# Gated linear attention into a three-way maxout FFN: weights by the fp32 queue in order of use with casts on three engines, the state update as its own stage, and a ring of one-bank PSUM slots

## The chip, the cores and the metric

The kernel runs on one core of one Trainium2 chip. Times are device microseconds of one execution. A run's time is 1.7 to 1.9 us longer than the span of its profile, which counts from the first to the last instruction. Executions of one kernel mostly agree within 1%. Engines are named as the profile names them: PE is TensorE's matrix multiplication (PEld its weight loads), DVE the vector engine, ACT the scalar engine, POOL the GpSimd engine, SP the engine that issues most transfers.

## The reference

```python
batch, n_heads, seq, head_dim = (4, 8, 768, 48)       # q, k, v, alpha
n_tokens, d_model, d_ff = (3072, 384, 768)            # w1, w2, w3, w_out

def _attn_ref(q, k, v, alpha):
    state = np.zeros((B, H, D, D)); y = np.zeros_like(q)
    for t in range(S):
        state = alpha[:, :, t, :, None] * state + np.einsum('bhd,bhe->bhde', k[:, :, t], v[:, :, t])
        y[:, :, t] = np.einsum('bhd,bhde->bhe', q[:, :, t], state)
    return y

def _moe_ref(x, w1, w2, w3, w_out):                   # x: y as tokens x 384
    h = np.maximum(np.maximum(x @ w1, x @ w2), x @ w3)
    return h @ w_out
```

Everything is given and returned in fp32; the kernel multiplies in fp16.

## The kernel before

Work is cut into 12 **units** of two batches by 128 tokens (all 8 heads): two pairs of batches by six blocks of time, the pairs in turn, so the state that a unit leaves is needed two units later. Each unit passes four steps, and I use these names throughout:

- **A**: logarithm of alpha (ACT), sums over time by matmul (`lps`), exponentials (ACT), and k, q, v scaled (POOL, DVE).
- **B**: k and q transposed on TensorE (`tps`) and copied by DVE (`qkT`), the score products k·q (`aps`), masked by DVE (`lat`), the outputs (`yps`), and their transposition (`xtp`).
- **C**: the new state (`sps`), multiplied by a product of gates (`gm`) into `st`. Before the change this is inside B.
- **FFN**: 54 matmuls of 256 columns (`gps`), two casts by ACT and two maxima by DVE for each third (`h`, `hT`), then 12 matmuls of 384 columns (`ops`).

PSUM is the memory that this kernel's matmuls write their results to; a slot is a piece of it that tiles of one tag take in turn. The kernel divides PSUM into four one-bank slots for `gps` (tag "g"), two for `xtp`, `yps`, `sps`, `ops` (tag "s"), and two more banks as ONE slot (tag "w") that `lps`, `tps` and `aps` share.

```python
    def load_weights():                       # POOL's queue; the transfer converts fp32 to fp16
        for jg in range(NJ // 2):
            for g, w in enumerate((moe_w1, moe_w2, moe_w3)):
                cs = slice(jg * 2 * P, (jg + 1) * 2 * P)
                nc.gpsimd.dma_start(
                    wcat[:, :, g, cs], w.rearrange("(f p) j -> p f j", p=P)[:, :, cs])
        nc.gpsimd.dma_start(wo16, moe_w_out.rearrange("(j p) m -> p j m", p=P))
# ... (stage_a cut)
    def stage_b(s):
        tps = ps.tile([P, 2 * NP, P], FP16, name="tps", tag="w", bufs=1)
        for i in range(2 * NP):
            nc.tensor.transpose(tps[:, i, :], qkf[:, i, :], ident)
        nc.vector.tensor_copy(out=qkT.rearrange("p i a t -> p (i a) t"), in_=tps)
        # ...
            for i in range(2):                # gate products
                nc.vector.scalar_tensor_tensor(
                    out=gm[:, :, i], in0=gate_of[s][:, :, 1], scalar=half_c[i],
                    in1=gate_of[s + B // U][:, :, 0], op0=AOP.mult, op1=AOP.mult)
        for u in range(U):                    # two batches
            aps = ps.tile([P, 2, HP, P], FP32, name="aps", tag="w", bufs=1)
            for p in range(HP):               # four pairs of heads
                for i in range(2):            # rows 0 to 47, rows 64 to 111
                    rows = slice(64 * i, 64 * i + D)
                    nc.tensor.matmul(aps[:, i, p, :], qkT[rows, 1, u * HP + p, :],
                                     qkT[rows, 0, u * HP + p, :], start=True, stop=True)
            # ... mask, yps, xb, xtp, and the state (sps, st)
# ...
    stage_a(0)
    load(1)
    load_weights()
    load(2)
    stage_a(1)
    stage_a(2)
    stage_b(0)
    for s in range(NS):
        if s + 3 < NS:
            load(s + 3)
            stage_a(s + 3)
        if s + 1 < NS:
            stage_b(s + 1)
        ffn(s)
```

The order in which an engine meets its instructions is set when the program is built, from this source and from which slots are free; it can differ from the source's order, and "program order" below means that built order. I read the traces as each engine taking its instructions in order; unit 0's transposes, below, are an example.

Of the kernel before, what the change touches and what calls it, by code (L numbers as in the profile page):

```python
# [12 lines left out]
AOP = mybir.AluOpType  # L13
# [10 lines left out]
def kernel(  # L24
# [43 lines left out]
    raw = ctx.enter_context(tc.tile_pool(name="raw", bufs=3))  # L68
# [12 lines left out]
    def load(s):  # L81
        cb, b0 = where(s)
        for n in ("a", "q", "k", "v"):
            t = raw.tile([P, NH, D], FP32, name=f"r{n}", tag=f"r{n}")
            nc.sync.dma_start(  # L85
                t, ins[n][cb * P:(cb + 1) * P, b0:b0 + U].rearrange("s b h d -> s (b h) d"))
            raws[s, n] = t
# [8 lines left out]
    half_c = (c32[:, 4:5], c32[:, 5:6])  # L96
# [5 lines left out]
    for i in range(NQ):  # L102
        nc.vector.memset(las[i], 0.0)
        nc.gpsimd.memset(qks[i], 0.0)
    sts = [[cpool.tile([P, HP, 2 * D], FP16, name=f"st{b}_{i}") for i in range(2)]
           for b in range(B)]

    wcat = cpool.tile([P, NF, 3, DF], FP16, name="wcat")
    wo16 = cpool.tile([P, NJ, DM], FP16, name="wo16")

    def load_weights():
        for jg in range(NJ // 2):
            for g, w in enumerate((moe_w1, moe_w2, moe_w3)):
                cs = slice(jg * 2 * P, (jg + 1) * 2 * P)
                nc.gpsimd.dma_start(
                    wcat[:, :, g, cs], w.rearrange("(f p) j -> p f j", p=P)[:, :, cs])
        nc.gpsimd.dma_start(wo16, moe_w_out.rearrange("(j p) m -> p j m", p=P))
# [3 lines left out]
    def stage_a(s):  # L121

        la, qk = las[s % NQ], qks[s % NQ]
        nc.scalar.activation(  # L124
            out=la.rearrange("p a b c -> p (a b) c")[:, :, :D], in_=raws.pop((s, "a")),
            func=AFT.Ln)
        lps = ps.tile([P, 2, 512], FP32, name="lps", tag="w", bufs=1)
        laf = la.rearrange("p a b c -> p (a b) c")
        for i in range(2):
            nc.tensor.matmul(lps[:, i, :H * D], tri, laf[:, i * H:(i + 1) * H, :D],  # L130
                             start=True, stop=True)
        for p in range(NP):
            nc.tensor.matmul(lps[:, 0, H * D + 2 * p:H * D + 2 * p + 2],  # L133
                             la[:, p].rearrange("p a b -> p (a b)"), w2,
                             start=True, stop=True)
        ac = work.tile([P, 2, H, D], FP32, name="ac", tag="ac")
        ic = work.tile([P, 2, H, D], FP32, name="ic", tag="ic")
        ge = work.tile([P, NP, 2], FP32, name="ge", tag="ge", bufs=6)
        lv = lps[:, :, :H * D].rearrange("p i (h d) -> p i h d", d=D)
        nc.scalar.activation(out=ac, in_=lv, func=AFT.Exp, bias=at_c, scale=1.0)  # L140
        nc.scalar.activation(out=ic, in_=lv, func=AFT.Exp, bias=nat_c, scale=-1.0)  # L141
        nc.scalar.activation(  # L142
            out=ge, in_=lps[:, 0, H * D:H * D + 2 * NP].rearrange("p (a b) -> p a b", b=2),
            func=AFT.Exp)
        gate_of[s] = ge
        qv, kv = (qk[:, i].rearrange("p a b c -> p (a b) c")[:, :, :D] for i in range(2))
        nc.vector.tensor_mul(qv, raws.pop((s, "q")), ac.rearrange("p i h d -> p (i h) d"))  # L147
        nc.gpsimd.tensor_mul(kv, raws.pop((s, "k")), ic.rearrange("p i h d -> p (i h) d"))  # L148
        vt = work.tile([P, NH, D], FP16, name="vt", tag="vt", bufs=4)
        nc.gpsimd.tensor_scalar_mul(vt, raws.pop((s, "v")), vs_c)  # L150
        qk_of[s], v_of[s] = qk, vt

    def stage_b(s):

        cb, b0 = where(s)
        qk, vt = qk_of.pop(s), v_of.pop(s)
        qkf = qk.rearrange("p i a b c -> p (i a) (b c)")
        tps = ps.tile([P, 2 * NP, P], FP16, name="tps", tag="w", bufs=1)
        for i in range(2 * NP):
            nc.tensor.transpose(tps[:, i, :], qkf[:, i, :], ident)  # L160
        qkT = work.tile([P, 2, NP, P], FP16, name="qkT", tag="qkT")
        nc.vector.tensor_copy(out=qkT.rearrange("p i a t -> p (i a) t"), in_=tps)  # L162
        xT = work.tile([P, NF, U, P], FP16, name="xT", tag="xT")
        xtp = ps.tile([P, U, NF, P], FP16, name="xtp", tag="s", bufs=2)
        gm = None
        if cb + 1 < NCB:
            gm = work.tile([P, NP, 2], FP32, name="gm", tag="gm")
            for i in range(2):
                nc.vector.scalar_tensor_tensor(  # L169
                    out=gm[:, :, i], in0=gate_of[s][:, :, 1], scalar=half_c[i],  # L170
                    in1=gate_of[s + B // U][:, :, 0], op0=AOP.mult, op1=AOP.mult)
        for u in range(U):
            b = b0 + u
            st, stn = sts[b][cb % 2], sts[b][(cb + 1) % 2]
            aps = ps.tile([P, 2, HP, P], FP32, name="aps", tag="w", bufs=1)
            for p in range(HP):
                for i in range(2):
                    rows = slice(64 * i, 64 * i + D)
                    nc.tensor.matmul(aps[:, i, p, :], qkT[rows, 1, u * HP + p, :],  # L179
                                     qkT[rows, 0, u * HP + p, :], start=True, stop=True)  # L180
            la_ = work.tile([P, 2, HP, P], FP16, name="lat", tag="lat")
            nc.vector.tensor_mul(  # L182
                la_.rearrange("p i a t -> p (i a) t"), aps.rearrange("p i a t -> p (i a) t"),
                mask.unsqueeze(1).broadcast_to([P, H, P]))
            yps = ps.tile([P, HP, 2, D], FP32, name="yps", tag="s", bufs=2)
            for p in range(HP):
                if cb > 0:
                    nc.tensor.matmul(yps[:, p], qkT[:, 0, u * HP + p, :], st[:, p, :],  # L188
                                     start=True, stop=False)
# [8 lines left out]
            if cb + 1 < NCB:  # L198
                sps = ps.tile([P, HP, 2, D], FP32, name="sps", tag="s", bufs=2)
                if cb > 0:  # L200
                    nc.tensor.matmul(sps.rearrange("p a b d -> p (a b d)"), ident,
                                     st.rearrange("p a b -> p (a b)"),
                                     start=True, stop=False)
                for p in range(HP):
                    nc.tensor.matmul(  # L205
                        sps[:, p], qkf[:, NP + u * HP + p, :],
                        vt[:, u * H + 2 * p:u * H + 2 * p + 2, :],
                        start=(cb == 0), stop=(cb == 0 or p == HP - 1))
                nc.vector.tensor_mul(
                    stn.rearrange("p a (b d) -> p a b d", d=D), sps,  # L210
                    gm[:, u * HP:(u + 1) * HP, :].unsqueeze(3).broadcast_to([P, HP, 2, D]))
        nc.scalar.copy(out=xT.rearrange("p f u t -> p u f t"), in_=xtp)
        xT_of[s] = xT

# [33 lines left out]
    stage_a(0)  # L248
    load(1)
    load_weights()  # L250
    load(2)
    stage_a(1)
    stage_a(2)
    stage_b(0)
    for s in range(NS):
        if s + 3 < NS:
            load(s + 3)
            stage_a(s + 3)
        if s + 1 < NS:
            stage_b(s + 1)  # L260
        ffn(s)
# [30 lines left out]
```

## Time and profile before

| | before |
|---|---|
| median of its runs (three, when the prediction was made) | 212.29 us (210.94 to 212.34) |
| span of the profile | 209.7 us |
| first FFN product starts | 47.6 us |
| end of FFN(0), FFN(4), FFN(11) | 61.5, 118.3, 206.0 us |
| one full iteration (mean of four, 105.5 to 161.8 us) | 14.08 us |

From the page of before, the busy shares, the overview (40 slices of 5.24 us; a digit is the busy share in tenths, PEclk the granted clock of TensorE in tenths) and the chain of waits:

```profile
PE 154.2 (74%) x1736; PEld 117.1 (56%) x1736; DVE 120.9 (58%) x164; ACT 104.1 (50%) x181; POOL 63.2 (30%) x42
...
PE   0110002469997989987699877899988999999992
...
PEclk9999999999999999999999999999999999999998
DMA  7999999999109959889179689500200102020012
...
SPq L85 8%; PE ops L241 7%; DMA ra<-in_alpha_dram 7%; DVE gm L169 4%; ACT xb L195 4%; ACT ac L140 3%; PE tps L160 3%; PE xtp L197 3%; DVE hT L237 3%; DVE qkT L162 3%; PE aps L179 3%; DVE lat L182 2%; PE yps L191 2%; PE yps L188 2%; PE sps L205 1%
```

TensorE does almost nothing for seven slices (37 us) while the transfer engines are full; two slices later it is 60 to over 90% busy. The order of time of TensorE at the end of that stretch (start, time, engine, line, operation, tile, count, and in brackets the idle time before and who ended it):

```profile
33.34 0.80 PE L130 MATMUL lps<-la_82,c_68 128*128 128x384 f16 x2 [18.26 <-ACT la_82 L124]
...
36.18 1.87 PE L160 MATMUL tps<-c_68,qk_84 128*128 128x128 f16 x16 [1.85 <-ACT ge L142]
...
47.62 0.37 PE L226 MATMUL gps_403<-xT,wcat 128*128 128x256 f16 x1 [0.65 <-ACT xT L212]
```

TensorE waits 18 us for the sums of unit 2, whose alpha lands at 32.4 us; unit 0's transposes, whose data are long there, stand behind them in the queue. The stretches of four later iterations (length, then busy time and number of instructions of PE, PEld, DVE, ACT and POOL, granted clock, share of the transfer engines, GB/s):

```profile
105.50:118.30 12.80, 12.03 (x141) 9.06 (x139) 8.21 (x11) 6.88 (x13) 3.60 (x2) 1.00 0.89 186
118.30:134.40 16.10, 13.23 (x161) 10.12 (x160) 11.54 (x17) 10.81 (x19) 4.37 (x3) 1.00 0.87 173
134.40:146.80 12.40, 11.98 (x140) 9.04 (x138) 7.86 (x11) 6.18 (x11) 3.63 (x2) 1.00 0.09 33
146.80:161.80 15.00, 13.21 (x163) 10.20 (x161) 12.13 (x16) 9.69 (x18) 2.80 (x2) 1.00 0.08 28
```

TensorE is busy 50.45 of these 56.3 us, so an iteration holds 12.6 us of it and 1.5 us of waits.

### The profile page before, as it was taken

To read this page: it belongs to the slowest core of one execution; us is meant where nothing else is said; L and a number is where in the kernel's file an instruction comes from. 1 tells how busy PE (TensorE), PEld (TensorE's weight loads), DVE (VectorE), ACT (ScalarE), POOL (GpSimd) and SP (SyncE) were. 2 spreads that over 40 slices of the span, in tenths; PEclk is the share of its full clock that TensorE was granted. 3 is DMA by queue.
4 is the path that set the end of the run, shared out by engine and by line. 5 is a ranking of instruction groups with operands and counts; after the bars stand their busy time and mean duration, and the time that the engine had idled before them with its cause. 6 is when DMAs were issued, how large, how long until landed. Compare 5 with 4: busy or idle time off the path is not lost.

```text
span 209.7 us, 4208 instructions
## 1 busy us (share of the span) xinstructions
PE 154.2 (74%) x1736; PEld 117.1 (56%) x1736; DVE 120.9 (58%) x164; ACT 104.1 (50%) x181; POOL 63.2 (30%) x42
## 2 busy tenths in 40 slices
PE   0110002469997989987699877899988999999992
PEld 0110002347676767675487665676766777767680
DVE  3101002755939888479857398475798865548250
ACT  2422004073567574684656556645748454644651
POOL 8997313607403434052330430704303000000000
PEclk9999999999999999999999999999999999999998
DMA  7999999999109959889179689500200102020012
GB/s 140 218 189 219 178 201 230 218 220 204 31 27 237 222 122 224 155 200 223 31 179 193 139 179 231 124 16 3 78 0 23 55 3 75 5 75 3 27 48 75
DMA packets 107219, 26.32 MB, mean 126 GB/s; under 512 B 99776, under 2 KB 107200, under 8 KB 107200
## 3 DMA queue, kind: packets, MB, share of 16 engines
q1 hardware_dynamic: 102528, 23.60, 56.9%
q0 software_dynamic: 4384, 2.36, 8.0%
q8 instruction: 13, 0.21, 0.4%
q10 hardware_dynamic: 288, 0.10, 0.3%
q14 instruction: 6, 0.05, 0.1%
HBM read 23.69 MB, written 4.72 MB: 136 GB/s over the span
## 4 chain that ended last, share of the span: by engine, by line
PE 45%; DVE 18%; ACT 15%; SPq 8%; DMA 7%; issue 5%; ACTq 0%; DVEq 0%
SPq L85 8%; PE ops L241 7%; DMA ra<-in_alpha_dram 7%; DVE gm L169 4%; ACT xb L195 4%; ACT ac L140 3%; PE tps L160 3%; PE xtp L197 3%; DVE hT L237 3%; DVE qkT L162 3%; PE aps L179 3%; DVE lat L182 2%; PE yps L191 2%; PE yps L188 2%; PE sps L205 1%
## 5 line engine op out<-in xcount | busy, mean ns | idle before, releaser
L226 PEld LDWEIGHTS <-wcat 128*128 128x128 f16 x648 | 60.1, 99 | 7.6
L150 POOL TENSOR_SCALAR vt<-rv,c_69 128x768 f16<-128x768 f32 x12 | 26.5, 2205 | 43.7 <-DMA rv<-in_v_dram 21.2
L182 DVE TENSOR_TENSOR lat<-aps,c_68 128x1024 f16<-128x1024 f32 x24 | 29.2, 1219 | 5.7 <-PE aps L179 5.7
L241 PE MATMUL ops<-wo_105,hT 128*128 128x384 f16 x144 | 26.7, 326 | 4.5 <-DVE hT L237 1.7
L241 PEld LDWEIGHTS <-hT 128*128 128x128 f16 x144 | 13.4, 98 | 14.7 <-DVE hT L237 4.7
L130 PEld LDWEIGHTS <-c_68 128*128 128x128 f16 x24 | 2.2, 100 | 32.4 <-issue 27.4
L244 ACT COPY ob<-ops 128x384 f32<-128x384 f32 x24 | 11.1, 480 | 17.9 <-PE ops L241 17.8
L162 DVE COPY qkT<-tps 128x2048 f16<-128x2048 f16 x12 | 14.6, 1220 | 8.6 <-PE tps L160 8.6
L195 ACT ACTIVATE xb<-yps,c_69 128x384 f16<-128x384 f32 x24 | 14.0, 582 | 10.9 <-PE yps L191 10.7
L169 DVE SCALAR_TENSOR_TENSOR gm<-ge,c_69 128x8 f32<-128x8 f32 x20 | 16.5, 862 | 1.3 <-ACT ge L142 1.1
L130 PE MATMUL lps<-la_82,c_68 128*128 128x384 f16 x6 | 1.8, 385 | 18.3 <-ACT la_82 L124 18.3
L147 DVE TENSOR_TENSOR qk_86<-rq,ac 128x768 f16<-128x768 f32 x3 | 2.9, 958 | 20.7 <-ACT ac L140 20.7
L140 ACT ACTIVATE ac<-lps,c_69 128x768 f32<-128x768 f32 x12 | 10.9, 905 | 7.1 <-PE lps L133 7.1
L179 PE MATMUL aps<-qkT 48*128 48x128 f16 x192 | 10.0, 226 | 6.0 <-DVE qkT L162 5.9
L191 PE MATMUL yps<-vt,lat 128*128 128x48 f16 x192 | 11.6, 187 | 1.6 <-DVE lat L182 1.5
L148 POOL TENSOR_TENSOR qk_87<-rk,ic 128x768 f16<-128x768 f32 x3 | 5.4, 1810 | 24.1 <-ACT ic L141 14.3
L197 PE MATMUL xtp<-c_68,xb 128*128 128x128 f16 x72 | 8.5, 229 | 5.0 <-ACT xb L195 3.3
L191 PEld LDWEIGHTS <-lat 128*128 128x128 f16 x192 | 9.6, 98 | 4.1 <-DVE lat L182 3.0
L179 PEld LDWEIGHTS <-qkT 48*128 48x128 f16 x192 | 5.6, 97 | 9.7 <-DVE qkT L162 9.0
L141 ACT ACTIVATE ic<-lps,c_69 128x768 f32<-128x768 f32 x12 | 10.8, 904 | 0.0
L124 ACT ACTIVATE la_82<-ra 128x768 f16<-128x768 f32 x3 | 2.6, 850 | 15.6 <-DMA ra<-in_alpha_dram 15.6
L197 PEld LDWEIGHTS <-xb 128*128 128x128 f16 x72 | 4.2, 100 | 10.7 <-ACT xb L195 10.5
(331 smaller groups left out, 333.0 us busy)
## 6 DMA issues: line engine op xcount, KB each, us to landing
ra<-in_alpha_dram SPq DMA_DIRECT2D x12, 384.0 KB, 5.7
rq<-in_q_dram SPq DMA_DIRECT2D x12, 384.0 KB, 5.7
rk<-in_k_dram SPq DMA_DIRECT2D x12, 384.0 KB, 5.7
rv<-in_v_dram SPq DMA_DIRECT2D x12, 384.0 KB, 5.8
out_dram<-ob SPq DMA_DIRECT2D x24, 192.0 KB, 1.9
wcat<-in_moe_w_dram POOLq DMA_DIRECT2D x9, 192.0 KB, 6.1
wo_105<-in_moe_w_out_dram POOLq DMA_DIRECT2D x1, 576.0 KB, 11.5
c_68<-c ACTq DMA_DIRECT2D x1, 96.5 KB, 2.7
```

The lines of the kernel that those rows point to most:

```text
L85: nc.sync.dma_start(t, ins[n][cb * P:(cb + 1) * P, b0:b0 + U].rearrange("s b h d -> s (b h) d"))
L140: nc.scalar.activation(out=ac, in_=lv, func=AFT.Exp, bias=at_c, scale=1.0)
L150: nc.gpsimd.tensor_scalar_mul(vt, raws.pop((s, "v")), vs_c)
L162: nc.vector.tensor_copy(out=qkT.rearrange("p i a t -> p (i a) t"), in_=tps)
L169: nc.vector.scalar_tensor_tensor(out=gm[:, :, i], in0=gate_of[s][:, :, 1], scalar=half_c[i], in1=gate_of[s + B // U][:, :, 0], op0=AOP.mul ...
L179: nc.tensor.matmul(aps[:, i, p, :], qkT[rows, 1, u * HP + p, :], qkT[rows, 0, u * HP + p, :], start=True, stop=True)
L182: nc.vector.tensor_mul(la_.rearrange("p i a t -> p (i a) t"), aps.rearrange("p i a t -> p (i a) t"), mask.unsqueeze(1).broadcast_to([P, H, ...
L191: nc.tensor.matmul(yps[:, p, i, :], la_[:, i, p, :], vt[:, u * H + 2 * p + i, :], start=(cb == 0), stop=(cb == 0 or i == 1))
L195: nc.scalar.mul(xb, yps.rearrange("p a b d -> p (a b d)"), ys_c)
L197: nc.tensor.transpose(xtp[:, u, f, :], xb[:, f * P:(f + 1) * P], ident)
L226: nc.tensor.matmul(gps[:, j, :], wcat[:, f, g, jj * P:(jj + 1) * P], xT[:, f].rearrange("p u t -> p (u t)"), start=(f == 0), stop=(f == NF ...
L241: nc.tensor.matmul(ops, hT[:, jj, u * P:(u + 1) * P], wo16[:, jj, :], start=(jj == 0), stop=(jj == NJ - 1))
```

## The change

Its intent: (1) stage B(0) and FFN(0) no longer stand behind three stages A and all loads; weights come in fp32 by the same queue as the inputs, cut in the order in which FFN(0) uses them, and ACT, DVE and POOL share the casts; (2) the state update is a stage C of its own, and its gate products go from DVE to POOL; (3) the two-bank slot becomes a ring of two one-bank slots, so that TensorE can fill one while DVE empties the other.

```diff
@@ weights
-                nc.gpsimd.dma_start(
-                    wcat[:, :, g, cs], w.rearrange("(f p) j -> p f j", p=P)[:, :, cs])
-        nc.gpsimd.dma_start(wo16, moe_w_out.rearrange("(j p) m -> p j m", p=P))
+                t = cpool.tile([P, NF, 2 * P], FP32, name=f"ws{jg}_{g}")
+                nc.sync.dma_start(t, w.rearrange("(f p) j -> p f j", p=P)[:, :, cs])
+                wstage.append((g, wcat[:, :, g, cs], t))
+        # ... w_out in three parts likewise; g = 0, 1, 2 is cast by ACT, DVE, POOL
@@ stage_a: one-bank sums per batch instead of one two-bank tile
-        lps = ps.tile([P, 2, 512], FP32, name="lps", tag="w", bufs=1)
+        for u in range(U):
+            lps = ps.tile([P, 512], FP32, name="lps", tag="w", bufs=2)
+            # ... sums, exponentials, and k, q scaled, per batch
@@ stage_b
-        tps = ps.tile([P, 2 * NP, P], FP16, name="tps", tag="w", bufs=1)
+        for u in range(U):
+            tps = ps.tile([P, 2, HP, P], FP16, name="tps", tag="w", bufs=2)
+            # ... eight transposes, one copy
-            aps = ps.tile([P, 2, HP, P], FP32, name="aps", tag="w", bufs=1)
+            aps = [ps.tile([P, HP, P], FP32, name=f"aps{i}", tag="w", bufs=2)
+                   for i in range(2)]
             for p in range(HP):
                 for i in range(2):
                     rows = slice(64 * i, 64 * i + D)
-                    nc.tensor.matmul(aps[:, i, p, :], qkT[rows, 1, u * HP + p, :], ...
+                    nc.tensor.matmul(aps[i][:, p, :], qkT[rows, u, 1, p, :], ...
+            for i in range(2):                    # two half masks instead of one
+                nc.vector.tensor_mul(la_[:, i], aps[i], mask...)
@@ stage_c, new: the state update, out of stage_b
+        gt = work.tile([P, NP], FP32, name="gt", tag="gt")
+        nc.gpsimd.tensor_mul(gt, gate_of[s][:, :, 1], gate_of[s + B // U][:, :, 0])
+        gm = work.tile([P, NP, 2], FP32, name="gm", tag="gm")
+        nc.gpsimd.tensor_mul(gm, gt..., half_c...)
+        # ... sps and st as before
@@ order
-    stage_a(0)
     load(1)
     load_weights()
     load(2)
+    load(3)
+    stage_a(0)
+    stage_b(0)
     stage_a(1)
-    stage_a(2)
-    stage_b(0)
+    cast_weights()
     for s in range(NS):
-        if s + 3 < NS:
-            load(s + 3)
-            stage_a(s + 3)
+        if s + 4 < NS:
+            load(s + 4)
         if s + 1 < NS:
             stage_b(s + 1)
+        if s + 2 < NS:
+            stage_a(s + 2)
+        stage_c(s)
         ffn(s)
```

(Also: k is loaded ahead of q, four input buffers instead of three, only the padding is cleared.)

## The prediction

> **What bounds the kernel now.** The 40-slice overview shows two regimes. Until about 47 us TensorE is mostly idle: the stretch table gives it 2.0 of the first 18 us, 0.7 of the next 16. Later it is the limit: 13.6 of 14 us at 160 to 174. The chain of waits explains the start: SyncE's issue of loads (8%), then 14.3 us for the third unit's alpha, until 32.45. The program queues stage A of units 0, 1 and 2 on TensorE ahead of the first stage B, so the first transposes, whose data were there by 13 us, run at 34.5 to 38, and the first FFN matmul at 47.6. An iteration with stage A takes 13.5 to 15 us, the last ones 11.7 to 12. In the order of time at 134.3 to 147.2 I count 12.2 us of real TensorE work in a full iteration, so 1.5 to 2 us are waits.
>
> **What changes.**
> 1. Start. Only unit 0's load precedes stage B(0); then unit 1; then weights. Before, units 0, 1 and all weights had landed by about 31 us, and the same bytes are read now, so I keep 32 us for the last weight. The Trainium skill ("DMA: Bandwidth & Descriptors", Issuing engines are not separate DMA queues) says all queues share the same 16 engines; the trace agrees: DMA share 0.9 or more in this time. The gain is not bandwidth but what TensorE does meanwhile: A(0), B(0), A(1), B(1), FFN(0)'s first products; FFN(1) stands ahead of unit 2.
> 2. Twelve casts of 128x768. The like-sized ACT logarithm takes 0.85 us, POOL's scaling 2.2: 4 us each on ACT, DVE, 6 to 9 on POOL, inside the load time, off the chain.
> 3. DVE loses the gate products (1.85 us a unit, 16.5 in all), which stand before the transposes' copy on the chain. POOL gets two small ones.
> 4. PSUM ring: two one-bank slots instead of one of two banks; copy and masks halved (1.22 us becomes 2 x 0.65), so TensorE fills one while DVE empties the other. State products leave the ring between the two heads' outputs.
> 5. ACT gets three more instructions per unit, some 0.5 us.
>
> TensorE's work is unchanged (3,474 rows in both orders).
>
> **Sum.** At 32 us FFN(0)'s first products are done. Left: one output product 2.1, 11 FFN at 8.05, ten B at 2.8, ten A at 0.55, ten C at 0.66: 131 us. Waits: 0.75 us x 11 = 8 (0.55 of each before the last output products: unchanged); 2 us of slow clock (early transposes take 117 ns, later 66); 7 us in units 2 to 4, whose stage B has no FFN matmuls between its steps; 3.7 after the last matmul. Span 184; the time runs 1 to 2.6 above: **185 us, range 177 to 193**. Faster by over 2%: 0.96; within: 0.03; slower: 0.01.
>
> **Right if:** first FFN matmul before 25 us, FFN(1)'s before 35; full iterations of 12.6 to 13.4 us; TensorE's busy share above 82%; last weight landed at 29 to 36 us; no gate products on DVE.
>
> **Wrong if:** weights land after 36 us; in-order casts hold up stage B; loads of units 2 to 5, now behind 4.7 MB of weights, starve TensorE at 40 to 60 us; POOL's casts slow down beside DVE's; or halved steps add more fixed cost than overlap, leaving iterations at 14 us (then about 194).

## The result, and the profile after

| | before | predicted | after |
|---|---|---|---|
| median | 212.31 us (4 runs) | 185 (177 to 193) | 197.27 us (196.82 to 197.89, 4 runs) |
| span of the profile | 209.7 | 184 | 195.0 |
| first FFN product | 47.6 | under 25 | 23.3 us |
| FFN(0)'s 54 products done | 59.1 | 32 | 35.4 us |
| end of FFN(4) | 118.3 | 95.6 (the same terms) | 101.9 us |
| full iteration | 14.08 | 12.8 | 13.86 us (five, from FFN(4) to FFN(9)) |
| last weight landed | 30.5 | 32 | 31.9 us |

The ratio to before is 0.930, 95% interval 0.924 to 0.936. Ratios here are the mean time of one kernel's fast runs over the mean of the other's fast runs of the same rounds, so they are not quite the ratios of the medians that I quote.

The change is faster by 7%, but 12 us slower than I said. FFN(4) ends 16.4 us earlier than before, FFN(11) 14.3 us: all of the gain is made at the start, and later iterations cost nearly what they did. The lines of the page that answer to those of before:

```profile
PE 167.9 (86%) x1736; PEld 122.5 (63%) x1736; DVE 116.8 (60%) x200; ACT 110.7 (57%) x221; POOL 61.2 (31%) x64
...
PE   0295886958869979999989999999989999999992
...
PEclk9999999996999988999999999999999999999999
DMA  7999999999996059379699909819720020020102
...
PE ops L267 7%; DVE hT L263 5%; PE tps L179 5%; ACT ic L157 4%; DMA rq<-in_q_dram 3%; SPq L85 3%; DMA ra<-in_alpha_dram 2%; ACT xb L208 2%; POOL vt L167 2%; POOL qk_86 L163 2%; ACT ac L158 2%; PE yps L204 2%; POOL gt L221 1%; DVE qkT L182 1%; PE xtp L210 1%
```

The first line is the surprise. TensorE runs the same 1,736 matmuls, and is busy 13.7 us longer. The gate products of DVE (4% of the old chain) are gone from it; the POOL that took them is in it.

The order of time of TensorE at the start, in after:

```profile
23.32 0.82 PE L252 MATMUL gps_437<-xT,wcat 128*128 128x256 f16 x3
...
32.55 0.83 PE L252 MATMUL gps_491<-xT,wcat 128*128 128x256 f16 x6 [0.75 <-ACT wcat L131]
33.94 0.83 PE L252 MATMUL gps_498<-xT,wcat 128*128 128x256 f16 x6 [0.55 <-DVE wcat L133]
...
44.43 3.72 PE L267 MATMUL ops<-wo_97,hT 128*128 128x384 f16 x12 [2.59 <-DVE st_1_89 L237]
```

FFN(0) starts when predicted, but waits for casts (2.0 us in all, with one at 28.8 and one at 30.2 us), although the weight behind the line at 32.55 had landed at 26.4 us: ACT made its cast at 31.66, in program order behind its own casts of FFN(0)'s products. FFN(0)'s last part, `ops`, comes 9 us after its products: it needs an output slot, and both are held by state products that wait for a gate of unit 2. Its 12 matmuls then take 3.7 us instead of 2.1.

The stretches of five full iterations in after:

```profile
101.90:115.80 13.90, 13.39 (x151) 9.71 (x149) 9.61 (x16) 8.71 (x19) 4.91 (x5) 1.00 0.75 156
115.80:129.40 13.60, 13.42 (x152) 9.75 (x150) 9.23 (x16) 9.77 (x20) 4.90 (x5) 1.00 0.68 146
129.40:144.30 14.90, 13.65 (x157) 10.11 (x155) 9.37 (x16) 8.74 (x19) 7.03 (x6) 1.00 0.68 135
144.30:157.60 13.30, 13.11 (x147) 9.46 (x145) 9.22 (x16) 8.33 (x18) 2.72 (x4) 1.00 0.08 31
157.60:171.20 13.60, 13.41 (x152) 9.75 (x150) 9.22 (x16) 8.28 (x18) 2.72 (x4) 1.00 0.08 30
```

Waits have nearly gone, as intended, but TensorE is now busy 13.4 us in each. To see with what, I added up every matmul's time from its start to the next one's start, less the gap after its recorded end (that gap is the wait). Per full iteration, in us; the last column is an experiment below:

| | predicted | before | after | all scores together |
|---|---|---|---|---|
| FFN products and outputs | 8.05 | 8.50 | 8.69 | 8.57 |
| B | 2.8 | 2.83 | 3.51 | 3.02 |
| of B, the scores `aps` | | 0.66 | 1.31 | 0.66 |
| A | 0.55 | 0.56 | 0.54 | 0.53 |
| C | 0.66 | 0.75 | 0.66 | 0.66 |
| waits | 0.75 | 1.46 | 0.46 | 1.10 |
| sum | 12.81 | 14.10 | 13.86 | 13.88 |

The scores take double the time with the same 16 matmuls. In before they come as two groups of eight, in after as four groups of four. A group of eight in before, then groups of four in after:

```profile
107.72 0.40 PE L179 MATMUL aps<-qkT 48*128 48x128 f16 x8
108.05 0.22 PE L188 MATMUL yps<-st_0_100,qkT 128*128 128x96 f16 x1
```

```profile
117.08 0.39 PE L193 MATMUL aps_1788<-qkT 48*128 48x128 f16 x4
117.40 0.22 PE L201 MATMUL yps<-st_1_93,qkT 128*128 128x96 f16 x1
...
117.88 0.40 PE L193 MATMUL aps_1789<-qkT 48*128 48x128 f16 x4
118.21 0.61 PE L252 MATMUL gps_1906<-xT,wcat 128*128 128x256 f16 x4
```

From the start of each group to the next matmul 0.32 to 0.33 us pass. A group of eight takes as long (108.05 less 107.72, and again in the first experiment). Each matmul uses 48 of the 128 rows, one half of the array; with both halves in one tile they run side by side, and with a one-bank tile for each half, in a ring of two slots, program order parts the halves. The Trainium skill ("TensorEngine Tiling (Array Packing)", Key Properties) says that tiles work independently and can multiply in parallel, and that "Changing tiling mode (not just tile) drains the TensorE". The traces agree as far as they go: in the group of eight two matmuls start 3 or 4 ns apart and the next two some 55 ns later, in the group of four each starts some 55 ns after the one before; in both, 0.15 us pass from the last start to the next product. That this last part is the draining, no run shows. Twice as many groups, twice the time.

So my **first theory** was: the time missing in full iterations is TensorE's, made by the parted scores (0.65 us an iteration, 6.5 us over ten), and the time missing at the start comes from the output slots held by C(0). The **rival**: TensorE's time is not what sets an iteration; waits would take the place of whatever it saved.

### The profile page after: what moved, and what is told of

Same layout as the page of the kernel before. It is cut to its first block, busy times and chain, and to the rows that moved or that the text cites. A ratio compares the mean times of both kernels' runs of the same rounds, so it can differ in the third digit from the quotient of the medians.

```text
span 195.0 us, 4340 instructions
## 1 busy us (share of the span) xinstructions
PE 167.9 (86%) x1736; PEld 122.5 (63%) x1736; DVE 116.8 (60%) x200; ACT 110.7 (57%) x221; POOL 61.2 (31%) x64
## 3 DMA queue, kind: packets, MB, share of 16 engines
q1 hardware_dynamic: 106944, 28.32, 67.5%
## 4 chain that ended last, share of the span: by engine, by line
PE 41%; DVE 16%; ACT 13%; issue 9%; POOL 9%; DMA 5%; SPq 4%; POOLq 0%; DVEq 0%; ACTq 0%
PE ops L267 7%; DVE hT L263 5%; PE tps L179 5%; ACT ic L157 4%; DMA rq<-in_q_dram 3%; SPq L85 3%; DMA ra<-in_alpha_dram 2%; ACT xb L208 2%; POOL vt L167 2%; POOL qk_86 L163 2%; ACT ac L158 2%; PE yps L204 2%; POOL gt L221 1%; DVE qkT L182 1%; PE xtp L210 1%
## 5 line engine op out<-in xcount | busy, mean ns | idle before, releaser
L267 PE MATMUL ops<-wo_97,hT 128*128 128x384 f16 x144 | 29.2, 342 | 6.1 <-DVE hT L263 2.9
L267 PEld LDWEIGHTS <-hT 128*128 128x128 f16 x144 | 13.5, 102 | 18.2 <-DVE hT L263 7.6
L182 DVE COPY qkT<-tps 128x1024 f16<-128x1024 f16 x24 | 15.6, 686 | 14.9 <-PE tps L179 14.9
L193 PEld LDWEIGHTS <-qkT 48*128 48x128 f16 x192 | 11.7, 100 | 9.8 <-DVE qkT L182 4.3
L204 PE MATMUL yps<-vt,lat 128*128 128x48 f16 x192 | 14.9, 189 | 0.5 <-DVE lat L196 0.2
L163 POOL TENSOR_TENSOR qk_86<-rk,ic 128x384 f16<-128x384 f32 x6 | 6.0, 997 | 28.6 <-ACT ic L157 28.6
L157 ACT ACTIVATE ic<-lps,c_69 128x384 f32<-128x384 f32 x24 | 14.0, 584 | 1.3 <-PE lps L151 1.1
L163 POOL TENSOR_TENSOR qk_87<-rk,ic 128x384 f16<-128x384 f32 x6 | 6.0, 997 | 26.6 <-ACT ic L157 26.6
L158 ACT ACTIVATE ac<-lps,c_69 128x384 f32<-128x384 f32 x24 | 14.0, 584 | 0.0
L163 POOL TENSOR_TENSOR qk_84<-rk,ic 128x384 f16<-128x384 f32 x6 | 6.2, 1039 | 21.2 <-ACT ic L157 21.2
L163 POOL TENSOR_TENSOR qk_85<-rk,ic 128x384 f16<-128x384 f32 x6 | 6.3, 1042 | 17.3 <-ACT ic L157 17.3
L211 ACT COPY xT<-xtp 128x768 f16<-128x768 f16 x12 | 9.6, 797 | 0.6 <-PE xtp L210 0.4
L164 DVE TENSOR_TENSOR qk_84<-rq,ac 128x384 f16<-128x384 f32 x6 | 4.8, 808 | 7.5 <-DMA rq<-in_q_dram 6.0
L201 PEld LDWEIGHTS <-qkT 128*128 128x128 f16 x80 | 7.6, 97 | 0.7
L164 DVE TENSOR_TENSOR qk_85<-rq,ac 128x384 f16<-128x384 f32 x6 | 4.6, 766 | 4.9 <-ACT ac L158 4.9
```

Of the source, the lines that this page charges most:

```text
L157: nc.scalar.activation(out=ic, in_=lv, func=AFT.Exp, bias=nat_c, scale=-1.0)
L158: nc.scalar.activation(out=ac, in_=lv, func=AFT.Exp, bias=at_c, scale=1.0)
L163: nc.gpsimd.tensor_mul(kv, rk[:, hs], ic)
L182: nc.vector.tensor_copy(out=qkT[:, u], in_=tps)
L193: nc.tensor.matmul(aps[i][:, p, :], qkT[rows, u, 1, p, :], qkT[rows, u, 0, p, :], start=True, stop=True)
L204: nc.tensor.matmul(yps[:, p, i, :], la_[:, i, p, :], vt[:, u * H + 2 * p + i, :], start=(cb == 0), stop=(cb == 0 or i == 1))
```

## The experiments

All kernels gave correct results. Ratios use fast runs alone; a median may include a slow one (one of four in e5_swdge). Medians of before in the five sets of rounds were 211.49, 212.16, 211.79, 212.80 and 212.66 us. After is 197.27 us, ratio 0.930.

### e2_seq: issue order of the halves, in the kernel before

```diff
-            for p in range(HP):
-                for i in range(2):
+            for i in range(2):
+                for p in range(HP):
```

> The kernel before, with one loop pair swapped: the eight score products of a head group are issued four with partitions 0 to 47 and then four with partitions 64 to 111, instead of alternating. Every engine has the same list of instructions; only which operands stand in the eight differs. Row-pairing theory (alternating products of the two partition halves overlap on TensorE, four of one half do not; in the trace of before eight took 0.33 us, after the change four take 0.33): each group of eight grows from 0.33 to about 0.65 us, 24 groups, so 6 to 8 us longer, 218 to 220 us. Rival (the longer score stage of the changed kernel comes from the two-slot ring and its semaphores, not from the order): same time within 1 us, about 212.

Measured: 211.76 us, ratio 1.003 (0.996 to 1.009). The profile, order of time:

```profile
107.69 0.41 PE L179 MATMUL aps<-qkT 48*128 48x128 f16 x8
108.03 0.22 PE L188 MATMUL yps<-st,qkT 128*128 128x96 f16 x1
```

Four of one half followed at once by four of the other (the built program has them in this order) still take 0.34 us, and their starts still come in pairs, 13 ns apart: they overlap. Alternation is not needed, adjacency is. What costs is other work between the halves.

### e4_twobank: two-bank tiles back, all else as after

```diff
-            tps = ps.tile([P, 2, HP, P], FP16, name="tps", tag="w", bufs=2)
+        tps2 = ps.tile([P, U, 2, HP, P], FP16, name="tps", tag="w", bufs=1)   # lps likewise
-            aps = [ps.tile([P, HP, P], FP32, name=f"aps{i}", tag="w", bufs=2) for i in range(2)]
+            aps2 = ps.tile([P, 2, HP, P], FP32, name="aps", tag="w", bufs=1)
```

> The changed kernel with the one-bank ring alone undone: the tiles of decay sums, transposes and scores are again two banks in a single slot, the halved copies, exponentials and masks stay. The eight score products then alternate again. Row-pairing theory: a group of eight takes 0.33 to 0.35 us, some 0.7 us less TensorE time a unit, iterations of about 12.8 us instead of 13.6, 187 to 191 us in all. Rival (the one-bank ring brought overlap that is worth keeping, and the long iterations have another cause): slower than the changed kernel's 197.3, 199 to 204.

Measured: 207.71 us, ratio 0.983 (0.977 to 0.989). From FFN(4) to FFN(9):

```profile
112.60:184.50 71.90, 65.04 (x750) 47.64 (x747) 47.36 (x81) 44.25 (x91) 20.00 (x23) 1.00 0.44 95
```

The scores are back at 0.66 us an iteration, and yet an iteration takes 14.38 us: waits rise from 0.46 to 1.37 us, 0.75 of it the output products', whose slot DVE's state product still holds, and the FFN's own work from 8.69 to 8.99 us. Undoing the ring costs 10 us, all of it by the end of FFN(4) (112.6 instead of 101.9 us); I had expected this kernel to be the faster one. Part of the 10 us is the clock (see e15_hold). A first warning that saved TensorE time and a shorter iteration are two things.

### e3_c0late, e8_clate, e7_both: the state update after the FFN

```diff
-        stage_c(s)                 # e8_clate: for all units; e3_c0late: for unit 0 alone
         ffn(s)
+        stage_c(s)                 # e7_both: e3_c0late with the two-bank tiles of e4_twobank
```

> The changed kernel with the state update of the first unit moved behind its FFN, for that unit alone. Slot theory (the two state products of unit 0 are computed at 29 to 31 us and hold both slots of the PSUM ring that the FFN outputs need, until the gate that needs unit 2's alpha arrives at 43.8; TensorE stands 2.4 us and then runs at half clock): first output products before 38 us instead of 44.4, no half-clock stretch at 44 to 48, 3 to 5 us less, 192 to 194. Rival (the start is bound by the arrival of units 2 and 3, so what is won early is waited for again): within 1 us of 197.3.

> The kernel after, with every state update placed after the feed-forward part of its unit instead of ahead of it. If the state products holding both slots of the output tag are what stops the feed-forward outputs in the first iterations (2.4 us idle at 42 to 44.4 us, then the half clock), FFN(0) ends at about 41 us and the end comes 2 us earlier, 194 to 196 us. Rival, after the run that moved only the first update (199.6 us): the time is given back in stage B(2), which has no filler; 198 to 201 us.

> Both edits together: two-bank ring and late state update of unit 0. If both theories hold and add up: 197.3 less 7 to 9 less 3 to 5, so 184 to 187 us. If either is wrong, its share is missing; if both touch the same stretch at 44 to 60 us, 188 to 190.

Measured: e3_c0late 199.64 us (ratio 0.944), e8_clate 199.41 us (0.942), e7_both 201.85 us (0.955). The wait for the slots goes: FFN(0) ends at 40.4 us with e3_c0late and 39.5 with e8_clate, instead of 48.2. But FFN(1) ends at 62.6 in e3_c0late instead of 59.7, and FFN(4) at 104.5 instead of 101.9. Taking out the wait that the trace shows most plainly made the kernel 2 us slower: in e3_c0late stage B(2), 47.4 to 54.6 us, has no FFN products left to stand between its steps, the last ones of FFN(1) come only after it and C(1), and the granted clock from 48 to 60 us is 0.58 (1.00 in after). That part of my theory fell. e7_both shows that the two edits do not add: with the slot of before, moving C(0) gains 6 us, in the ring it loses 2.

### e10_alpha: alpha of units 2 and 3 loaded ahead of the weights

```diff
     load(1)
+    load(2, ("a",))
+    load(3, ("a",))
     load_weights()
     # ... then load(2) and load(3) with k, q and v alone
```

> The changed kernel with the alpha loads of units 2 and 3 moved ahead of the weights in the one load queue; nothing else is edited. Queue-order theory (unit 2's alpha lands at 33.2 us, but its logarithm stands behind ten casts of FFN products in ScalarE's program order and runs at 39.3; unit 3's lands at 41.6 and runs at 48.6; the gate, the state product, the PSUM slot and the FFN's output wait for it in turn): with the alphas there by 18 to 22 us the program order puts both logarithms before FFN(0); FFN(0)'s outputs end before 41 us instead of 48, FFN(2)'s before 71 instead of 77, and the whole gains 5 to 9 us, 188 to 192. Rival (the start is bound by bytes: units 2 to 4 arrive no sooner, and the weights later by 3 to 4 us): within 2 us of 197.3 or slower.

Measured: 196.80 us, ratio 0.931 (0.926 to 0.937), as after. FFN(0) ends at 43.5 us, FFN(4) at 101.2. The early gate gains 5 us and loses them by FFN(1) (62.4 instead of 59.7 us). The rival was right about the time, and the last weights land some 4 us later, as it said; but FFN(0)'s first product also comes at 28.8 us instead of 23.3, in a changed program order, so that bytes alone set the time is not shown.

### e5_swdge and e6_gate: two parts of the change undone

e5_swdge puts the converting transfers of before into after. e6_gate puts the gate products back on DVE:

```diff
-        nc.gpsimd.tensor_mul(gt, gate_of[s][:, :, 1], gate_of[s + B // U][:, :, 0])
-        nc.gpsimd.tensor_mul(gm, gt..., half_c...)
+        for i in range(2):
+            nc.vector.scalar_tensor_tensor(
+                out=gm[:, :, i], in0=gate_of[s][:, :, 1], scalar=half_c[:, i:i + 1],
+                in1=gate_of[s + B // U][:, :, 0], op0=AOP.mult, op1=AOP.mult)
```

> The changed kernel with the weights alone loaded as before: by GpSimd's queue, cast on the way, no staging and no casts on the engines. If the fp32 queue in order of use matters: the weights compete with units 0 and 1 from the start, stage A(0) ends later, and GpSimd's issues hold up its key products: 3 to 8 us slower than 197.3. If only the order of the stages matters: within 2 us of 197.3.

> The changed kernel with the gate products alone moved back to VectorE (two small products with a per-partition scalar a unit instead of two on GpSimd). Prediction's step 3 (VectorE's gate products cost 1.85 us a unit on the chain): 2 to 8 us slower than 197.3. Rival (in the new order VectorE has room, and GpSimd's products stand behind its key products in program order, 1 to 2 us late): same within 1.5 us, or up to 2 us faster.

Measured: e5_swdge 199.66 us, ratio 0.941 (0.937 to 0.945): the fp32 queue with casts is worth about 2.4 us, although FFN(0)'s first product comes at 32.3 us in this kernel and at 23.3 in after. Nine microseconds of head start shrink to two. e6_gate 198.02 us, ratio 0.934 (0.929 to 0.939): no difference from after that these runs show.

### e9_ring3 and e12a_own: other divisions of PSUM

e9_ring3 gives the ring three slots and the FFN products three; e12a_own gives the scores a two-bank slot of their own, leaves one slot for `lps` and `tps`, and three for the FFN products.

> The changed kernel with three one-bank slots for decay sums, transposes and scores, and three instead of four for the FFN products. Visit theory (one visit of TensorE to the half-array score products takes 0.33 us whether it makes four or eight; the two-slot ring makes four visits of a unit's two): the program order has three visits of a unit, so 0.2 to 0.3 us less a unit, and tiles wait less for a slot: 1 to 4 us faster than 197.3. Rival (the fourth FFN slot is worth more): 2 to 6 us slower.

> The kernel after, with a two-bank slot of its own for the scores of both halves, one one-bank slot left for the logarithm sums and transposes, and three slots instead of four for the feed-forward products. Two visits per unit of 8 score matmuls. Visit theory alone: scores at 0.66 us a unit, 0.6 us off each iteration, 190 to 193 us. Rival (slots decide): one slot for transposes makes them wait for DVE's copy as before the change, and three slots for the feed-forward products hold TensorE; 198 to 205 us.

Measured: e9_ring3 198.01 us (0.933), e12a_own 197.71 us (0.935); neither differs from after. In e12a_own the scores are at 0.66 us an iteration and a full iteration takes 13.72 us instead of 13.86: 0.5 us less work, 0.4 us more waits. Its start is not better (FFN(4) ends at 103.7 us), with TensorE at half clock for 13.7 us of it, 6.8 in after.

### e12g_scores: all scores of a unit together, the ring kept

```diff
-            aps = [ps.tile([P, HP, P], FP32, name=f"aps{i}", tag="w", bufs=2)
-                   for i in range(2)]
+            aps = [ps.tile([P, HP, P], FP32, name="aps0", tag="w", bufs=2),
+                   ps.tile([P, HP, P], FP32, name="aps1", tag="g", bufs=4)]
```

One line: the second half's tile takes one of the FFN products' slots. In the built program the halves now stand together.

> The kernel after, with the second head half's score tile taken from the four slots of the feed-forward products instead of the two-slot ring. The score products of both halves then alternate and stand together in the program (one visit of TensorE per unit of two batches, instead of four), and the ring stays for everything else. Visit theory: a visit costs 0.33 us whether it holds 4 or 8 matmuls, so the score products fall from 1.3 us a unit to 0.7 or less, full iterations from 13.9 to about 13.2 us, the last feed-forward part ends at 184 to 187 us, and the time is 189 to 192 us, ratio to before about 0.90. Rival (TensorE was not short of time there; what sets an iteration is the chain copy, scores, mask, outputs, or the slots): score products shrink, but the time stays at 196 to 199 us because idle or other products' waits grow by the same amount.

Measured: **191.29 us** (190.69 to 192.47, 6 runs), ratio 0.904 (0.900 to 0.909), 6 us faster than after. The time I had expected, and not for my reason. FFN(4) ends at 96.0 us instead of 101.9, and from there to FFN(9) both kernels take 69.3 us. First after, then e12g_scores, over those 69.3 us:

```profile
101.90:171.20 69.30, 66.98 (x744) 48.78 (x742) 46.65 (x80) 43.84 (x90) 22.28 (x24) 1.00 0.46 101
```

```profile
96.00:165.30 69.30, 63.82 (x744) 47.21 (x742) 49.60 (x80) 42.81 (x90) 22.17 (x24) 1.00 0.45 98
```

The same 744 matmuls, 3.2 us less of TensorE, not a tenth of a microsecond less of time. The order of time shows one of the waits that came in:

```profile
138.26 1.06 PE L179 MATMUL tps<-c,qk 128*128 128x128 f16 x16
139.66 0.40 PE L193 MATMUL aps<-qkT 48*128 48x128 f16 x8 [0.34 <-DVE qkT L182]
```

The scores wait 0.34 us for DVE's copy of the transposes. In after, three FFN products stand in that gap (116.57 us in its trace); here they do not, as I read it because the FFN's next slot is given after the scores' slot. The same order has another effect at the start: FFN(1)'s products wait for the scores of B(2), so that they fill B(2) instead of running ahead of it.

This run therefore mixed two things at the start: fewer groups of scores, and FFN(1) held back. The runs e18_start_only, e19_steady_only and e15_hold, below, part them.

### e13_g_clate and e16_copy_act: e12g_scores with one thing more

e13_g_clate puts the state updates after the FFN as well; e16_copy_act gives the second batch's copy of the transposes to ACT instead of DVE.

> Both at once: scores' second half in the feed-forward slots and the state updates after the feed-forward part. If the two add up and each is worth what its theory says, 187 to 190 us; if only the visits count, 189 to 192 us; if neither, 197 to 201 us.

> All units' scores in the feed-forward slots, and the copy of the second batch's transposes moved from DVE to ACT. In the run without it TensorE waited 0.34 us in each full iteration for the copy ahead of the scores, and 0.41 us for DVE's maximum ahead of the last output products; DVE is busy 9.8 and ACT 8.1 us of 13.5. If DVE's chain makes these waits, iterations fall from 13.9 to 13.2 to 13.6 us and the time to 186 to 189 us, a version that beats all so far. If they are fixed latencies or ACT becomes the queue that holds them, 190 to 193 us.

Measured: e13_g_clate 197.27 us (0.932), e16_copy_act 193.23 us (0.911). e13_g_clate is slower than e12g_scores; for e16_copy_act that is not clear, since the intervals overlap (0.905 to 0.917 against 0.900 to 0.909), but it is no gain. In e16_copy_act the 0.34 us ahead of the scores stays (the first copy is still DVE's), and 0.2 us more appear ahead of the second batch's scores.

### e18_start_only, e19_steady_only: scores together in the first five units, or in the others

```diff
+            other = ("g", 4) if s < 5 else ("w", 2)          # e19_steady_only: s >= 5
             aps = [ps.tile([P, HP, P], FP32, name="aps0", tag="w", bufs=2),
-                   ps.tile([P, HP, P], FP32, name="aps1", tag="g", bufs=4)]
+                   ps.tile([P, HP, P], FP32, name="aps1", tag=other[0], bufs=other[1])]
```

> The kernel after with the scores' second half in the feed-forward slots for the first five units alone; the steady units have four visits as in after. In the profiles of the run with all units changed, full iterations took 13.86 us as in after, with 0.64 us less TensorE work and 0.64 us more waits. If so, this run shows the whole gain: FFN(4) at 96 us, time 190.5 to 193 us. If the steady units carry part of it, 194 to 196 us.

> The other half: two whole-unit visits for units 5 to 11 alone, the start as in after. By the same reading nothing is gained: FFN(4) at 101 to 102 us, full iterations 13.8 to 13.9 us, 196 to 198 us. If fewer visits do shorten a full iteration, as I expected of the run with all units changed, 192 to 194 us.

Measured: e18_start_only 192.58 us, ratio 0.907 (0.901 to 0.913); e19_steady_only 197.35 us, ratio 0.931 (0.924 to 0.937). The start carries the gain, and whole groups in the later units alone gain nothing. In e19_steady_only, from FFN(4) to FFN(9):

```profile
102.30:171.30 69.00, 63.85 (x744) 47.27 (x742) 49.45 (x80) 42.84 (x90) 22.11 (x24) 1.00 0.47 101
```

3.1 us less TensorE time than in after, 0.3 us less time. The rival is right for full iterations, as long as the gates come late (see e24_scores_gate).

### e15_hold: FFN(1) held back, scores still parted

```diff
-            tps = ps.tile([P, 2, HP, P], FP16, name="tps", tag="w", bufs=2)
+            tps = ps.tile([P, 2, HP, P], FP16, name="tps", tag="wg"[u], bufs=(2, 4)[u])
```

> The kernel after, with the second batch's transposes (not scores) taken from the feed-forward slots. As in the fastest run so far, FFN(1) must now wait for stage B(2) and fills it, but the score products stay cut into three or four visits. If the start's gain of 6 us came from FFN(1) filling B(2), FFN(4) ends at 96 to 98 us and the time is 191 to 194 us. If it came from the fewer visits, the end stays at 101 us and the time at 196 to 199 us.

Measured: 194.84 us, ratio 0.918 (0.912 to 0.924), between the two. FFN(4) ends at 100.4 us. So of the 5.9 us that e12g_scores gains by then, holding FFN(1) back gives 1.5; the other 4.4 appear only where the scores are together as well. (The two do not hold it back alike: FFN(1) starts at 47.4 us here and at 44.8 in e12g_scores.) Added up from FFN(0)'s first product in after (23.3 us) to the end of FFN(4), TensorE's idle time is the same in after, e15_hold, e18_start_only and e12g_scores (9.5, 8.9, 9.6 and 9.9 us), while its work is 69.1, 68.2, 64.2 and 62.8 us. Of the 6.3 us between the first and the last, 3.2 are the scores themselves. At the start, then, TensorE time saved is time saved. Scores together without FFN(1) held back, in the same slots, I did not build.

A part of that work is slow clock, which I had overlooked. The granted clock of after, e12g_scores, e3_c0late and e4_twobank, in this order:

```profile
PEclk9999999996999988999999999999999999999999
PEclk9999999969999999999999999999999999999999
PEclk9999999999559997999999999999999999999998
PEclk9999999996757999999996999999999999999998
```

By the profiles' clock records, which begin at 25 to 30 us, TensorE is at half clock up to the end of FFN(4) for 6.8 us in after and in e15_hold, 3.4 in e12g_scores and e18_start_only, 13.7 in e3_c0late and 17.1 in e4_twobank. A busy TensorE loses half of such a time. So at most 1.7 of the 6 us that e12g_scores gains can be clock, but up to 5 of the 10 us that e4_twobank loses, and all of the 2 us of e3_c0late. No run parts the clock from the waits that stand beside it.

### e24_scores_gate and e25_scores_vact: the long ones among the full iterations

Full iterations are not equal: in after, 14.9 us stands among 13.3 to 13.9, in e12g_scores 14.8 and 14.1 among 13.5. The order of time of POOL in after's long one, and of TensorE at its end:

```profile
134.91 1.00 POOL L163 TENSOR_TENSOR qk_85<-rk,ic 128x384 f16<-128x384 f32 x1 [7.70 <-ACT ic L157]
135.89 2.50 POOL L167 TENSOR_SCALAR vt<-rv,c_69 128x768 f16<-128x768 f32 x1
138.37 0.99 POOL L163 TENSOR_TENSOR qk_85<-rk,ic 128x384 f16<-128x384 f32 x1
139.32 0.20 POOL L221 TENSOR_TENSOR gt<-ge 128x8 f32<-128x8 f32 x1
139.60 0.21 POOL L223 TENSOR_TENSOR gm<-gt,c_69 128x16 f32<-128x16 f32 x1
```

```profile
142.22 1.15 PE L267 MATMUL ops<-wo_97,hT 128*128 128x384 f16 x6 [1.23 <-DVE hT L263]
```

In this one iteration program order puts a 2.5 us scaling of v between the two products of k. The gate is late by as much; DVE's queue, which must multiply the state by it (1.60 us of idle time, ended by `gm`), holds the maxima that stand behind; the last FFN outputs wait for them. e24_scores_gate is e12g_scores with the gate products of e6_gate. e25_scores_vact is e12g_scores with

```diff
-        nc.gpsimd.tensor_scalar_mul(vt, raws.pop((s, "v")), vs_c)
+        if s < 2:
+            nc.gpsimd.tensor_scalar_mul(vt, raws.pop((s, "v")), vs_c)
+        else:
+            nc.scalar.mul(vt, raws.pop((s, "v")), vs_c)
```

> All units' scores in the feed-forward slots and the gate products back on DVE as before the change. In the run with POOL's gates one or two full iterations of 14.1 to 14.8 us stand among those of 13.5: there the gate came late on POOL (behind a scaling of v put ahead of it), DVE's in-order queue waited 2.6 us for it, and the last maximum and the output products with it. If that is what the long iterations are, they go, and the five from FFN(4) to FFN(9) sum to 67.5 instead of 69.3 us: 189 to 190 us. Rival: DVE, busy 9.8 of 13.5 us, gets 1.7 us more per unit in the same queue and every iteration pays 0.2 to 0.4: 190.5 to 193 us.

> All units' scores in the feed-forward slots, and the scaling of v moved from POOL (2.2 us) to ACT (about 0.85 us by the like-sized logarithm) for units 2 to 11; POOL keeps the gates, which now stand directly behind the second product of k. If late gates make the long iterations, these go without a burden on DVE: 67.5 us from FFN(4) to FFN(9), 188.5 to 190.5 us, the fastest of all. Rival: ACT's queue (8.1 of 13.5 us busy) delays the casts of the feed-forward products and each iteration pays it: 191 to 194 us.

Measured: e24_scores_gate 190.60 us, ratio 0.900 (0.895 to 0.905); e25_scores_vact **190.45 us** (189.77 to 190.67, 6 runs), ratio 0.898 (0.894 to 0.902). In both the long iterations are gone; in e25_scores_vact all five take 13.5 or 13.6 us:

```profile
97.40:164.90 67.50, 63.64 (x745) 47.39 (x743) 48.26 (x80) 45.84 (x94) 13.12 (x20) 1.00 0.45 101
```

That is the 1.8 us I expected there. The start gave most of it back (FFN(4) ends at 97.4 instead of 96.0 us), so the intervals of these two and of e12g_scores touch: that they beat it by a few tenths is not shown. That the late gate made the long iterations is: it was removed in two unlike ways, and both times the five iterations fell from 69.3 to 67.5 or 67.7 us. One run I had not set beside these: e6_gate, which has the prompt gates and parted scores. From FFN(4) to FFN(9) it takes

```profile
102.00:171.00 69.00, 66.86 (x740) 48.61 (x738) 49.04 (x90) 43.81 (x91) 19.06 (x14) 1.00 0.45 99
```

So in these profiles, one of each kernel, neither whole scores alone (69.0 to 69.3 us) nor prompt gates alone (69.0) shorten the five iterations of after (69.3) by more than 0.3 us, and both together by 1.6 to 1.8.

## Why the prediction was right or wrong, point by point

The predicted span was 183.7 us (the terms of its sum), the measured one 195.0. Until the end of FFN(4) 6.3 us were missed (101.9 against 95.6, which is 32 + 2.1 + 4 x 8.05 + 4 x 2.8 + 5 x 0.55 + 5 x 0.66 + 4 x 0.75 + 2 + 7), and 5.0 after it. Of the 6.3, 3.4 stand at FFN(0)'s last product; the rest, and the 5.0, are TensorE's work, while its waits were put too high.

- **"First FFN matmul before 25 us", right** (23.3), **FFN(1)'s "before 35", nearly** (35.3), **last weight at 29 to 36 us, right** (31.9), **TensorE busy above 82%, right** (86%) **and for a bad reason**: it is busy because the same matmuls take longer, not because the program is shorter. **No gate products on DVE, right.** **Faster by over 2%, right.**
- **"At 32 us FFN(0)'s first products are done", wrong by 3.4 us.** I took the last landing as the time of the last product. All parts of w1, w2 and w3 had landed by 28.7 us; the trace shows 2.0 us of waits for casts that stood in ACT's and DVE's queues behind FFN(0)'s own work, and its first products ran slower (six took 1.46 us at 25.90 us, 0.81 at 27.39). I had named in-order casts as a danger for stage B, where they did no harm; they were themselves held up. No run took this wait away alone, so its worth is read from the trace, not shown.
- **"TensorE's work is unchanged (3,474 rows in both orders)", wrong.** This is the step of the prediction that failed. I compared lists of instructions, and those are indeed the same in number; but the order decides which of them run side by side. B was put at 2.8 us an iteration and took 3.51, 0.65 of it the parted scores. FFN was put at 8.05, a length I had read from the last unit, where nothing stands between its products; in a full iteration it is 8.69 (8.50 before). The sum of work was therefore 13.40 us instead of 12.06. Of these 1.34 us, 0.58 stood in before already (12.64) and I had measured them too small; 0.76 came with the change. Five full iterations are 6.7 us of work longer than put, and 1.4 of waits shorter: that is the 5.0 us missed after FFN(4).
- **"Waits: 0.75 us x 11", wrong as a step, not only in size.** It was measured at 0.46 us, better than predicted. But I added waits to work as if each were a constant. e12g_scores and e19_steady_only took 0.6 us of work from each iteration and got 0.6 us of waits in exchange. A second limit of nearly the same length lies under TensorE's: 13.5 us with whole scores and prompt gates, of which TensorE works 12.7. The prediction of 12.8 had no room for it. What sets that 13.5 is open: the copy ahead of the scores is 0.34 us of it, and giving half of the copies to ACT did not shorten it.
- **"7 us in units 2 to 4" for stages B without fillers, plus 2 us of slow clock: the waits put high enough, the work beside them too low.** From FFN(0)'s last product (35.4 us) to the end of FFN(4) I had put 10 us of waits (7 and 4 x 0.75) and 53.6 of work, slow clock included; the trace has 7.5 and 59.0. The scores are 5.5 us there, against 2.6 at the pace of before, and TensorE is at half clock for 3.4 us from 44.3 and again from 71.6 us. It runs `ops` of FFN(0) in 3.7 us instead of 2.1, after 2.6 us of idling; the overview shows the granted clock at 6 and 8 tenths in three slices. The Trainium skill ("TensorE: Matmul & The Clock Gate", Part 1) puts the idle clock at half speed, and the half-speed matmuls of this trace agree (0.32 us from start to start instead of 0.16). With whole scores and FFN(1) held behind B(2) FFN(4) ends 5.9 us earlier.
- **Step 3, the gate products off DVE, worth nothing.** In e6_gate they are back on DVE without a loss that the runs show. On POOL they made one iteration of after some 1.2 us longer, but taking that away pays only where the scores stand together.
- **Step 4, the ring: right in its main effect, with a price I did not see.** Undoing it costs 10 us (e4_twobank), of which up to 5 can be slow clock; in full iterations its waits fell from 1.46 us before to 0.46. It also is what parted the scores.
- **The fallback in "wrong if", "halved steps add more fixed cost than overlap, leaving iterations at 14 us (then about 194)", was the nearest to what happened**, in size and in place. I gave it too little weight.
- The skill's statement I rested step 1 on ("DMA: Bandwidth & Descriptors", Issuing engines are not separate DMA queues) held: with one queue instead of two the last weight lands at 31.9 us against 30.5. What after gains on e5_swdge, 2.4 us, I put down to the order and to the queue's rate (284 to 357 GB/s in the slices in which mostly weights come), not to a second path; e5_swdge undoes queue, order and casts together, so this is argued and not shown.

## What to carry to other kernels

When a change splits a tile, look at the built program for small matmuls that used to stand side by side on different rows of the array: it is adjacency, not their count or their alternation, that lets them overlap. Do not add "work" and "waits" as two constants: before you bank a saving on the busy engine, ask what the next limit is and whether it is more than that saving away; one run with the saving in the late iterations alone answers it. Compare the granted clock of two runs before you put their difference down to waits. And put short products that release an in-order queue (here a gate of 0.2 us) ahead of long independent ones (here a scaling of 2.5 us) on the engine that makes them; here that paid only once the scores stood together.

## What the Trainium skill lacked or had wrong

- "TensorEngine Tiling (Array Packing)", Key Properties: it says that a change of tiling mode drains TensorE, but gives no cost. Here a group of four score products on one half of the array and a group of eight on both halves both took 0.32 to 0.34 us up to the next product, so parting two halves cost 0.33 us each time.
- The same page does not say what the order of issue must be for two tiles to overlap. Four of one half followed by four of the other, in the built program too, took 0.34 us for eight, as alternation did (0.33): adjacency is enough here.
- "TensorE: Matmul & The Clock Gate", Part 1: it warns that the clock's trace events are not to be relied on, but not that a stretch before the first of them can read as full clock. The stretches give a granted clock of 1.00 from 0 to 34 us, while three FFN products at 23.3 us took 0.82 us and later ones of the same shape 0.49.
- "DMA: Bandwidth & Descriptors", Specifications: it names 512 bytes as the least transfer for full rate; the page has an overhead for smaller pieces, but no measured rate of loads in them on this chip. Inputs in pieces of 192 bytes came at about 220 GB/s, weights in pieces of 1 KB at 284 to 357. The section SWDGE vs HWDGE vs iDMA says that casts in transfers need the GpSimd queue, but not what they cost against casts by engines: here the fp32 queue, its order and the casts together gained 2.4 us of the whole kernel, with casts of 0.8 to 0.95 us each (one of DVE's 0.55) for 128 by 768 elements on ACT, DVE and POOL (I had estimated 1.5 to 2.2 on POOL).
- No page that I used says that instructions of one engine can lose more from their order behind one another than from their length; the late gate (two products of 0.2 us, 1.2 us lost in an iteration) is such a case.
